# Batch 0 of a fused attention and softplus MLP: plain products, w_in stored once in fp32, fewer loads, and a new order of steps

## The chip, the cores and the metric

One core of one Trainium2 chip runs the whole program. The metric is device time in microseconds for one execution, the median of several runs. The core has five engines with a queue of instructions each: PE (TensorE, matrix products), DVE (VectorE) and ACT (ScalarE) for work on elements, POOL, and SP, which here issues nearly all DMA transfers. Each engine takes its instructions strictly in order and waits at an instruction until what it needs is there, so the order in which the program was written decides who waits for whom.

## What is computed

```python
# x (8,8,512,64), state (8,8,32,64); per batch and head
scores = scale * x @ state.T;   a  = softmax(scores);   xread = a @ state     # (512, 64)
scores2 = scale * state @ x.T;  a2 = softmax(scores2);  sread = a2 @ x        # (32, 64)
rows = concat([xread, sread])          # heads side by side: (8 * 544, 512)
h = rows @ w_in                        # (4352, 2048), w_in 512 x 2048
g = softplus(h)
out = g @ w_out                        # w_out 2048 x 512
```

The weights arrive as 64-bit floats and are turned into fp32 on the chip. An fp32 product is made from rounded parts (fp32r): each operand is split into a high part and a remainder, and three products high*high, high*low, low*high are summed.

## The kernel before

The first 512 rows of a batch (`xread`) go through the MLP batch by batch; the 32 `sread` rows of all eight batches form a ninth batch, number 8. `xread` itself is not built: `h = a @ (state @ w_in)`, so each batch has state products `V.b.c` (c is one of four column chunks of w_in, made by `B.V...`) and hidden tiles `h.b.f` (f = 0 to 15, 128 rows of hidden units by 512 tokens, six matmuls each: two groups of heads by three part products). For batches 4 to 7 the state products are made stacked (`B.K...`), written to DRAM (`vd`) and read back rearranged (`Lv`).

The second product runs as sweeps: batch b, half s of 256 tokens. A sweep has eight units u (two hidden tiles each), and a unit is a 2x2 block product with seven products in place of eight: `sfa`, `sfb`, `sfc` on DVE build sums of softplus blocks, `gh` (ACT) and `gl` (DVE) split seven blocks of 128 columns (896 wide) into parts, and `p.b.s.u.0` to `.3` are the PE steps (three of six 128x256 matmuls into the PSUM tiles `pk_X`, `pk_Y`, `pk_Z`, one of a 512- and a 256-wide matmul into `pk_Q`). `e1` to `e6` combine the banks and `So` stores the rows. W_out must be put in its own seven forms first (`cfa` to `cfd`, `wh`/`wl`, `Th`/`Tl`, `Eh`/`El`).

The softplus values of batches 0 to 7 are written to DRAM in whole tiles (`Td`, buffer `td`) and read back per sweep (`Tr`). For `sread`, each group of heads g of a batch has row maxima (`E`), exponentials (`e`), a transpose on DVE (`H`), a store (`Se`, buffer `te`), four rearranging loads per group (`Le.b.g.j`), two loads of x (`Lx`, from `in_xn`), and then the reads `B.Rb` on PE (tile `rp`). Batch 8 needs w_in itself in parts: `uh`/`ul` split it, `Su` stores the two parts (buffer `ud`), `Lu` loads them again before `h.8`.

The order of everything is the table `PLAN`: one entry `name:engine:place` per step, emitted one by one, so each engine's queue is this order with the other engines left out. `place` numbers PSUM banks or slots of SBUF. `w.i` are warm-up transposes of no use to the result. The helper lines are L323 (ACT copies and casts of `split` and `copy`), L339 (DVE subtractions of `split`), L330 and L333 (loads, stores), L342 (matmuls of `mm`), L736, L737, L740 (products of a sweep).

Of the kernel before, what the change touches and what calls it, by code (L numbers as in the profile page):

```python
# [42 lines left out]
PLAN = """
Lt.0.1:S:16 Lt.0.0:S:18 Lz.0:S:20 Li.0.0:S:22 Li.0.1:S:24 Lt.1.1:S:26 Lz.1:S:21 Lt.1.0:S:28 Li.0.3:S:30 Li.0.2:S:32 Li.1.3:S:34 Li.1.0:S:36 B.Q0:T:0,1
qk.0.0.0:A:38 qk.0.0.1:V: qk.0.1:A:39 w.0:T:3 A2.0.0:T:2 Sq.0.0:S: ch.0.0:A:40 Sq.0.1:S: ch.0.1:A:41 cu.0.0:V:42 Li.1.1:S:44 A.0.1:T:3 cr.0.0:V: A2.0.1:T:4
M.0.1:V: A.0.0:T:5 cu.0.1:V:46 Li.1.2:S:48 Ms.0.1:T: M.0.0:V: cr.0.1:V: Ms.0.0:T: m.0.1:A:50 N.0.1:V: V.0.0.0.0:T:6,7 m.0.0:A:51 V.0.0.0.1:T: ch.0.3:A:52
N.0.0:V: B.Q1:T:0,1 vf.0.0:A:53 vf.1.0:A:54 ch.0.2:A:55 Nm.0.1:V: qk.1.1:A:56 Nm.0.0:V: w.1:T:2 w.2:T:2 D.0.1:T:3 qk.1.0:A:57 Sq.1.1:S: cu.0.3:V: D.0.0:T:5
ch.1.3:A:58 Li.2.0:S:60 cu.0.2:V: A.1.1:T:4 ac.0.1:V:59 Li.2.1:S:62 ac.0.0:A:64 A.1.0:T:2 Sq.1.0:S: M.1.1:V: ch.1.0:A:65 h.0.1.0:T:1 cr.0.2:V: ah.0.0:A:66
Lq.0.1:S:68 h.0.1.1:T: ah.0.1:A:70 Ms.1.1:V:69 uh.0.0:A:72 cr.0.3:V: h.0.0.0:T:0 m.1.1:A: M.1.0:V: ch.1.1:A:55 h.0.0.1:T: N.1.1:V: s.0.0.1:A:74 V.0.0.1.0:T:
Ms.1.0:V:52 V.0.0.1.1:T: Nm.1.1:V: B.V1.0:T:3,5 vf.0.1:A: vf.1.1:V: m.1.0:A: cu.1.0:V:76 Li.2.2:S:78 h.0.2.0:T:4 cu.1.1:V: Li.2.3:S:80 cr.1.0:V: h.0.2.1:T:  # L50
cr.1.1:V: vh.1.0.0:A:82 N.1.0:V: h.0.3.0:T:2 vh.1.0.1:A:84 ch.1.2:A:65 h.0.3.1:T: E.0.1:V: s.0.0.0:A: D.1.1:T:1 Nm.1.0:V: vl.1.0.0:V: D.1.0:T:6 vl.1.0.1:V:
ah.1.1:A:86 Td.0.0:S: cu.1.2:V:88 ah.1.0:A:90 Li.3.0:S:92 al.1.1:V: s.0.1.0:A:94 al.1.0:V: s.0.1.1:A: cu.1.3:V: Li.3.1:S:96 ch.2.0:C:69 h.1.2:T:7 cr.1.2:V:
Td.0.1:S: ch.2.1:C:16 cr.1.3:V: ch.2.2:C:17 h.1.3:T:3 Lo.0:S:18 al.0.0:V: s.1.1.0:A:22 Lo.1:S:24 al.0.1:V: ch.2.3:C:40 cu.2.0:W:26 Li.3.2:S:28
B.V0.1+V1.1:T:0,5,1,4 ch.3.0:C:41 cu.2.1:W: Li.3.3:S:30 s.1.1.1:A: uh.0.1:A:32 Td.1.1:S: cr.2.0:V: ch.3.1:C:50 h.1.1:T:6 Lt.2.0:S:38 cr.2.1:V: vh.1.1.0:A:36
Lt.2.1:S:44 cu.2.2:W:56 Lt.3.0:S:54 vh.1.1.1:A:52 Lt.3.1:S:48 vh.0.1.0:A:34 vl.1.1.0:V: h.1.0:T:2 Lz.2:S:51 vh.0.1.1:A:64 vl.1.1.1:V: Lk.0:S:69 s.1.0.1:A:74
# [879 lines left out]
```

## Time and profile before

| what | us |
|---|---|
| median of 3 runs (lowest, highest) | 662.86 (662.17, 666.21) |
| the profiled execution, its own time | 663.22 |
| its span, from the first to the last instruction | 661.4 |
| PE busy in it, matmuls | 622.9 (94%) |
| DVE busy | 515.6 (78%) |
| ACT busy | 389.2 (59%) |
| moved by DMA | 157.88 MB, 239 GB/s on average |

PEld in the rows below is PE's loading of weights. Busy time of PE counts matmuls from their start to a modelled end, and neighbours overlap; the cost of one matmul in a stream is the distance between two starts. Idle time of an engine counts only where the work that ends last waits for it.

### The profile page before, as it was taken

Reading aid. Unit: us, or ns where it says so; the run is one execution under the profiler, and the core shown is the slowest. Engines: PE = TensorE matmul, PEld = TensorE weight load, DVE = VectorE, ACT = ScalarE, POOL = GpSimd, SP = SyncE. Lnnn points to the kernel's source line nnn. Section 1 sums busy time; section 2 is a strip of 40 time slices with the busy share of each in tenths; the row PEclk is TensorE's granted clock in tenths of the full one; section 3 lists DMA queues with packets and bytes.
Section 4 is the critical chain, followed back from the end, with each engine's and each line's share of the span. In section 5 each row is a group of like instructions: output and inputs, shape, how many; then the busy total and the mean of one; then the engine's idle time right before and its main releaser. Section 6 shows DMA issues by size and latency. Waiting matters only on the chain.

```text
span 661.4 us, 12889 instructions
## 1 busy us (share of the span) xinstructions
PE 622.9 (94%) x4710; PEld 540.1 (82%) x4710; DVE 515.6 (78%) x1126; ACT 389.2 (59%) x622; POOL 1.0 (0%) x7
## 2 busy tenths in 40 slices
...
PEclk9999999998999998999897999999999999999999
...
GB/s 332 334 383 412 358 300 367 374 348 368 343 310 145 203 223 228 271 189 255 229 208 218 170 230 218 197 224 169 182 218 231 251 211 159 224 203 35 145 48 33
DMA packets 73599, 157.88 MB, mean 239 GB/s; under 512 B 9536, under 2 KB 19776, under 8 KB 73536
## 3 DMA queue, kind: packets, MB, share of 16 engines
...
q10 hardware_dynamic: 288, 0.66, 0.3%
...
## 4 chain that ended last, share of the span: by engine, by line
PE 51%; DMA 21%; DVE 16%; ACT 5%; issue 3%; SPq 3%; DVEq 0%; ACTq 0%
PE pk_X L740 11%; PE h L342 10%; PE pk_Y L740 10%; PE pk_Z L740 10%; DVE arena L339 7%; DMA arena<-in_w_in_dram 4%; DMA arena<-in_xn_dram 4%; PE pk_Q L736 3%; ACT arena L323 3%; DMA arena<-td 2%; SPq L330 2%; PE h L794 2%; DMA vd<-arena 2%; DMA arena<-vd 2%; DMA td<-arena 2%
## 5 line engine op out<-in xcount | busy, mean ns | idle before, releaser
L323 ACT CAST arena<-arena 128x896 fp32r<-128x896 f32 (+2 forms) x231 | 180.4, 805 | 188.9 <-DVE arena L721 99.4
L339 DVE TENSOR_TENSOR arena<-arena,arena 128x896 fp32r<-128x896 f32 (+2 forms) x231 | 206.3, 912 | 56.5 <-ACT arena L323 53.7
L342 PE MATMUL h<-arena,arena 128*128 128x512 f32 x760 | 194.1, 404 | 10.4 <-ACT arena L693 4.0
L342 PEld LDWEIGHTS h<-arena,arena 128*128 128x128 f32 x760 | 140.3, 191 | 54.7 <-ACT arena L323 7.1
L740 PE MATMUL pk_Y<-arena,arena 128*128 128x256 f32 x816 | 122.0, 285 | 4.3 <-ACT arena L323 3.8
L740 PE MATMUL pk_X<-arena,arena 128*128 128x256 f32 x816 | 121.5, 285 | 0.2 <-DVE arena L339 0.2
L740 PE MATMUL pk_Z<-arena,arena 128*128 128x256 f32 x792 | 119.7, 287 | 0.4 <-DVE arena L747 0.4
L740 PEld LDWEIGHTS pk_X<-arena,arena 128*128 128x128 f32 x816 | 110.3, 191 | 9.6 <-ACT arena L323 0.8
L740 PEld LDWEIGHTS pk_Y<-arena,arena 128*128 128x128 f32 x816 | 108.6, 192 | 5.3 <-ACT arena L323 4.2
L740 PEld LDWEIGHTS pk_Z<-arena,arena 128*128 128x128 f32 x792 | 106.3, 194 | 2.0 <-issue 1.2
L718 DVE TENSOR_TENSOR arena<-arena 128x256 f32<-128x256 f32 x136 | 56.6, 420 | 48.0 <-DMA arena<-td 45.3
L693 ACT ACTIVATE arena<-h 128x512 f32<-128x512 f32 x128 | 74.5, 609 | 21.1 <-PE h L342 16.1
L736 PE MATMUL pk_Q<-arena,arena 128*128 128x512 f32 x128 | 51.5, 403 | 0.2 <-DVE arena L339 0.2
L721 DVE TENSOR_TENSOR arena<-arena 128x128 f32<-128x128 f32 x136 | 38.3, 287 | 1.6
L720 DVE TENSOR_TENSOR arena<-arena 128x128 f32<-128x128 f32 x136 | 37.9, 285 | 1.2
L737 PE MATMUL pk_Q<-arena,arena 128*128 128x256 f32 x128 | 36.0, 281 | 0.0
L342 PE MATMUL rp<-arena,arena 128*32 128x64 f32 x512 | 13.2, 266 | 15.4 <-DMA arena<-te 10.2
L342 PEld LDWEIGHTS rp<-arena,arena 128*32 128x32 f32 x512 | 10.9, 139 | 17.9 <-DMA arena<-te 10.3
L736 PEld LDWEIGHTS pk_Q<-arena,arena 128*128 128x128 f32 x128 | 24.6, 192 | 0.6 <-DVE arena L339 0.4
L737 PEld LDWEIGHTS pk_Q<-arena,arena 128*128 128x128 f32 x128 | 24.6, 192 | 0.0
L693 ACT ACT_TABLE_LOAD x18 | 23.1, 1283 | 1.5 <-PE h L342 1.2
L794 PE MATMUL h<-sreadT,arena 128*128 128x512 f32 x64 | 23.0, 393 | 0.0
...
## 6 DMA issues: line engine op xcount, KB each, us to landing
td<-arena SPq DMA_DIRECT2D x64, 512.0 KB, 4.4
arena<-td SPq DMA_DIRECT2D x128, 256.0 KB, 3.7
arena<-in_w_in_dram SPq DMA_DIRECT2D x16, 512.0 KB, 8.1
arena<-in_w_out_dram SPq DMA_DIRECT2D x16, 512.0 KB, 7.6
ud<-arena SPq DMA_DIRECT2D x16, 512.0 KB, 5.2
...
arena<-vd SPq DMA_DIRECT2D x128, 64.0 KB, 3.4
arena<-in_xn_dram SPq DMA_DIRECT2D x16, 512.0 KB, 6.8
```

The source lines that it names most:

```text
L323: nc.scalar.copy(dst, src)
L330: op(name, "S", list(ins), outs, lambda e: (nc.scalar if name in BYACT else nc.sync).dma_start(dst(), src()))
L339: lambda e: eng(e).tensor_tensor(r(dlo()), src(), dhi(), ALU.subtract))
L342: nc.tensor.matmul(dst, lhs, rhs, start=start, stop=stop)
L693: nc.scalar.activation(t[:, :, 0::3] if i == 0 else t[:, :, 1:3], src.rearrange("p (s c t) -> p s c t", s=2, t=P), AF.Softplus)
L718: op(f"sfa.{k}", "V", t, [f"t.{k}:a"], lambda e, g=blocks: nc.vector.tensor_tensor(g()[:, 0:2], g()[:, 4:7:2], g()[:, 7:8].broadcast_to([P ...
L720: op(f"sfb.{k}", "V", [t[0], f"t.{k}:a"], [f"t.{k}:b"], lambda e, g=blocks: nc.vector.tensor_tensor(g()[:, 2], g()[:, 1], g()[:, 4], ALU.add))
L721: op(f"sfc.{k}", "V", [t[1], f"t.{k}:b"], [f"t.{k}:c"], lambda e, g=blocks: nc.vector.tensor_tensor(g()[:, 3], g()[:, 5], g()[:, 2], ALU.s ...
L736: nc.tensor.matmul(at(bank), g(0), r(wform(u, m)(slice(0, 2))), start=first, stop=False, skip_group_check=True)
L737: nc.tensor.matmul(at(bank)[:, 0:256], g(1), r(wform(u, m)(0)), start=False, stop=True, skip_group_check=True)
L740: nc.tensor.matmul(at(bank)[:, 256 * half:256 * half + 256], g(gi), r(wform(u, m)(wi)), start=first and pi == ps[0] and i == 0, stop=i == ...
L794: nc.tensor.matmul(hb, r(w[:, 0, cs]), r(at("sreadT")[:, :, kt, :]), start=kt == 0, stop=False, skip_group_check=True)
```

## The change

Batch 0 no longer uses sweeps. Its hidden tiles are softened in one ACT instruction each (`s.0.f`), split (`gh.0.f`, `gl.0.f`, 512 wide, buffer `g`), kept in SBUF, and multiplied plainly: `m.0.f.c` adds three 128x512 matmuls to the accumulator of 128 rows c, in two turns (f 0 to 3, f 4 to 15); after the first the four accumulators are copied out (`o.0.0.c`), after the second added (`o.0.1.c`) and stored. Batch 0's `Td` and `Tr` are gone. Since the plain product needs W_out unchanged, `T1` is now split into W_out's slot after its last plain use (`Wh`, `Wl`), eight halves more.

w_in goes to DRAM as fp32 (`Sf`, buffer `fd`, eight stores of 512 KB) instead of as two parts (`Su`), is loaded in eight loads (`Lf`) and split again (`xh`, `xl`) for batch 8. `Le` loads both groups of a batch at once (32 issues where there were 64), `Lv` both halves of a chunk (64 where there were 128). `B.R0+R1` and `B.R2+R3` are taken apart. All steps are in a new order.

```diff
-SPILLED = (0, 1, 2, 3, 4, 5, 6, 7)
+SPILLED = (1, 2, 3, 4, 5, 6, 7)
+PLAIN = (0,)
+TURNS = ((0, 0, 4), (0, 4, 16))
-SWEEPS = tuple((b, s) for b in range(B) for s in range(2)) + ((8, 0),)
+SWEEPS = tuple((b, s) for b in range(B) if b not in PLAIN for s in range(2)) + ((8, 0),)
...
-                for j in range(4):
-                    load(f"Le.{k}.{j}", [f"aT.{k}:{j}"], lambda k=k, j=j: page(f"aT.{k}", 4, P)[NS * j:NS * j + NS],
-                         lambda k=k, j=j: io.te[k].rearrange("(q t) (j e) -> j t q e", t=NS, j=4)[j], [f"D:te.{k}"])
+                if g:
+                    for j in range(4):
+                        load(f"Le.{b}.{j}", [f"aT.{b}:{j}"], lambda b=b, j=j: page(f"aT.{b}", 8, P)[NS * j:NS * j + NS],
+                             lambda b=b, j=j: io.te[b].rearrange("g (q t) (j e) -> j t (g q) e", t=NS, j=4)[j], [f"D:te.{b}.{h}" for h in range(2)])
...
+        if PLAIN:
+            used = [f"acc.{b}.{x}.{c}:{f1}" for b, x, f0, fe in RUNS if f0 <= f1 < fe for c in range(4)]
+            split(f"Wh.{u}", f"Wl.{u}", lambda c1=c1: part(c1, 1), lambda f1=f1: page(f"W.{f1}", 2, DM)[:, 0, 256:512],
+                  lambda f1=f1: page(f"W.{f1}", 2, DM)[:, 1, 256:512], [f"{c1}:T"] + used, f"W.{f1}:Th", f"W.{f1}:Tl", "A")
...
+            def gemm2(e, acc=acc, c=c):
+                for i, (gi, wi) in enumerate(PASSES):
+                    mm(at(acc), r(page(f"g.{k}", 2, S)[:, gi, P * c:P * c + P]), r(page(f"W.{f}", 2, DM)[:, wi]), f == f0 and i == 0, f == f1 - 1 and i == 2)
...
+            store(f"Sf.{c}.{i}", whole, lambda c=c, i=i: io.fd[c, i], lambda c=c, i=i: at(f"wf.{c}.{i}"), [f"D:fd.{c}.{i}"])
+            load(f"Lf.{c}.{i}", [f"wg.{c}.{i}:"], lambda c=c, i=i: at(f"wg.{c}.{i}"), lambda c=c, i=i: io.fd[c, i], [f"D:fd.{c}.{i}"])
...
-            store(f"Su.{k}", [f"u.{k}:h", f"u.{k}:l"], lambda c=c, q=q: io.ud[c][q], lambda k=k: at(f"u.{k}"), [f"D:ud.{k}"])
-            load(f"Lu.{k}", [f"uu.{k}:h", f"uu.{k}:l"], lambda k=k: at(f"uu.{k}"), lambda c=c, q=q: io.ud[c][q], [f"D:ud.{k}"])
+            split(f"xh.{k}", f"xl.{k}", lambda c=c, q=q: page(f"wg.{c}.{q // 2}", 2, 512)[:, q % 2],
+                  lambda k=k: page(f"uu.{k}", 2, 512)[:, 0], lambda k=k: page(f"uu.{k}", 2, 512)[:, 1], [f"wg.{c}.{q // 2}:"], f"uu.{k}:h", f"uu.{k}:l", "A")
```

Where the order moves work, three places. The first is PE's queue early in the program, behind the hidden tiles 0 and 1 of batch 0 (`h_2`, `h_3` are tiles 2 and 3; `vp` are state products, `ab` are transposes of the softmax, `acc_0_c` the accumulators of the first turn). Before:

```order
L342 MATMUL h_2_418<-arena_356,arena_301 128x512
L342 MATMUL h_2_418<-arena_343,arena_317 128x512
L342 MATMUL h_3_431<-arena_356,arena_301 128x512
L342 MATMUL h_3_431<-arena_343,arena_317 128x512
L436 MATMUL ab_1_440<-ident,arena_371 128x128 x4
L436 MATMUL ab_0_447<-ident,arena_301 128x128 x4
L342 MATMUL h_2_471<-arena_458,arena_426 128x512 x3
```

Now:

```order
L331 MATMUL h_3_398<-arena_298,arena_288 128x512
L331 MATMUL acc_0_3_407<-arena_384,arena_389 128x512 x3
L331 MATMUL h_3_398<-arena_317,arena_288 128x512
L331 MATMUL acc_0_3_407<-arena_334,arena_402 128x512 x3
L331 MATMUL acc_0_1_428<-arena_384,arena_389 128x512 x3
L331 MATMUL acc_0_1_428<-arena_334,arena_402 128x512 x3
L331 MATMUL acc_0_0_440<-arena_384,arena_389 128x512 x3
L331 MATMUL acc_0_3_407<-arena_425,arena_419 128x512 x3
```

The sixteen plain products of the first turn have moved in between, and the hidden tiles of batch 1 (the last row of before) come behind them. The second place is where the last hidden tiles of batch 3 end on PE. Before, tiles of batch 4 and then batch 0's first unit follow:

```order
L342 MATMUL h_7_1904<-arena_1423,arena_573 128x512 x3
L342 MATMUL h_7_1904<-arena_1233,arena_1519 128x512 x3
L740 MATMUL pk_0_X<-arena_773,arena_1698 128x256 x3
L740 MATMUL pk_0_X<-arena_841,arena_1698 128x256 x3
L740 MATMUL pk_0_Y<-arena_773,arena_1698 128x256 x3
L740 MATMUL pk_0_Y<-arena_841,arena_1698 128x256 x3
```

Now the second turn, 48 rows of accumulators `acc_1_c` of which the first two and the last stand here, and then batch 1's first unit:

```order
L331 MATMUL h_15_1793<-arena_1170,arena_1223 128x512 x3
L331 MATMUL h_15_1793<-arena_594,arena_1223 128x512 x3
L331 MATMUL acc_1_0_1805<-arena_1619,arena_870 128x512 x3
L331 MATMUL acc_1_1_1815<-arena_1619,arena_870 128x512 x3
...
L331 MATMUL acc_1_3_1827<-arena_1978,arena_1967 128x512 x3
L766 MATMUL pk_0_X<-arena_384,arena_2025 128x256 x3
```

All hidden tiles of batch 4 have moved behind this point. The third place is SP's queue ahead of the reads of batches 0 and 1 (`te` numbers are per batch and group before, per batch now). Before, from the store of batch 1's second group to the last load of the pair of reads:

```order
L333 DMA te_69<-arena_2766 128x512
L330 DMA arena_1856<-te_67 32x4x128 x2
L330 DMA arena_285<-td_114 128x512
L330 DMA arena_1856<-te_67 32x4x128 x2
L330 DMA arena_1112<-in_xn_dram 128x1024
L330 DMA arena_2766<-in_xn_dram 128x1024
L330 DMA arena_2534<-in_xn_dram 128x1024
L330 DMA arena_1856<-te_66 32x4x128 x2
L330 DMA arena_1950<-in_xn_dram 128x1024
L330 DMA arena_1856<-te_66 32x4x128 x2
L330 DMA arena_414<-te_68 32x4x128 x4
L330 DMA arena_414<-te_69 32x4x128 x4
```

Now, the same from batch 1's second store to the loads of its own read:

```order
L322 DMA te_67<-arena_2338 128x512
L319 DMA arena_2347<-td_101 128x512
L319 DMA arena_767<-in_xn_dram 128x1024
L319 DMA arena_330<-in_xn_dram 128x1024
L319 DMA arena_2338<-te_67 32x8x128 x4
```

Batch 0's loads now stand earlier, before batch 1's stores, with a read of their own.

## Rows read from the trace of the kernel before

**Rows 1.** Page, span in 40 slices: granted PE clock in tenths.
```profile
PEclk9999999998999998999897999999999999999999
```
**Rows 2.** By stage: busy (x) of PE, PEld, DVE, ACT, POOL; PEclk, DMA, GB/s.
```profile
0.00:33.50 33.50, 28.10 (x186) 16.85 (x186) 23.72 (x51) 24.00 (x40) 1.01 (x7) 1.00 0.90 331
33.50:157.70 124.20, 116.64 (x718) 79.14 (x718) 100.77 (x204) 106.66 (x197) 0.00 (x0) 0.98 0.97 364
157.70:427.40 269.70, 248.43 (x2060) 225.46 (x2059) 219.79 (x505) 164.11 (x246) 0.00 (x0) 0.95 0.70 233
427.40:661.40 234.00, 229.68 (x1751) 218.66 (x1749) 171.32 (x370) 94.42 (x142) 0.00 (x0) 1.00 0.50 166
```
**Rows 3.** PE timeline at 442 us: start, us, line, operation, count [idle before <-releaser].
```profile
442.70 0.89 PE L740 MATMUL pk_X<-arena,arena 128*128 128x256 f32 x6
443.42 0.88 PE L740 MATMUL pk_Y<-arena,arena 128*128 128x256 f32 x6
...
444.86 0.40 PE L736 MATMUL pk_Q<-arena,arena 128*128 128x512 f32 x1
445.10 0.28 PE L737 MATMUL pk_Q<-arena,arena 128*128 128x256 f32 x1
445.21 1.56 PE L342 MATMUL h<-arena,arena 128*128 128x512 f32 x6
446.61 0.86 PE L740 MATMUL pk_X<-arena,arena 128*128 128x256 f32 x6
```
**Rows 4.** PE timeline at 33 us: the pair B.V0.1+V1.1 and what follows.
```profile
33.54 1.95 PE L342 MATMUL vp<-arena,arena 64*32 64x512 f32 x32
35.42 2.79 PE L342 MATMUL h<-arena,arena 128*128 128x512 f32 x11
```
**Rows 5.** Chain that ended last, pieces in order of time: start, us, what.
```profile
122.95 1.59 PE vq L342 x12
...
398.12 1.02 PE sc L342 x16
...
418.18 1.03 PE rp L342 x64
```
**Rows 6.** PE timeline: first product of batch 4, and the last products of all.
```profile
427.39 0.88 PE L740 MATMUL pk_X<-arena,arena 128*128 128x256 f32 x6
...
656.57 0.52 PE L740 MATMUL pk_Q<-arena,arena 128*128 128x256 f32 x3
```
**Rows 7.** PE timeline at batch 0's first product and around PE's waits.
```profile
168.94 0.88 PE L740 MATMUL pk_X<-arena,arena 128*128 128x256 f32 x6
...
195.68 0.38 PE L740 MATMUL pk_Y<-arena,arena 128*128 128x256 f32 x1 [3.79 <-ACT arena L323]
...
258.02 0.28 PE L737 MATMUL pk_Q<-arena,arena 128*128 128x256 f32 x1
...
265.72 1.66 PE L342 MATMUL h<-arena,arena 128*128 128x512 f32 x6
...
308.79 0.88 PE L740 MATMUL pk_Y<-arena,arena 128*128 128x256 f32 x6
...
316.93 1.44 PE L740 MATMUL pk_Z<-arena,arena 128*128 128x256 f32 x5
...
340.37 0.88 PE L740 MATMUL pk_Y<-arena,arena 128*128 128x256 f32 x6
...
351.52 1.65 PE L740 MATMUL pk_Z<-arena,arena 128*128 128x256 f32 x6
```
**Rows 8.** Tile rp (reads): what its engine waited for, us in total, times.
```profile
  DMA arena<-te: 20.5, 9
```
**Rows 9.** Page, DMA issues: count, KB each, us from issue to landing.
```profile
td<-arena SPq DMA_DIRECT2D x64, 512.0 KB, 4.4
...
ud<-arena SPq DMA_DIRECT2D x16, 512.0 KB, 5.2
```
**Rows 10.** SP's queue ahead of the reads R0+R1: start, us, issues merged.
```profile
254.03 8.06 SPq L330 DMA_DIRECT2D arena<-te  x10
```

More of the change, by code (lines that the diff above doesn't have):

```diff
@@ L48 @@
[L48 to L55, printed above, removed]
@@ L276 @@
+p.7.1.7.4:T: e4.7.1:V: e5.7.1:V: So.7.1.0:S: e7.7.1:V: So.7.1.1:S: e6.7.1:V: So.7.1.2:S: So.7.1.3:S:
 """
@@ L296, in width @@
     kind = buf.split(".")[0]
-    if kind in ("vp", "sc", "st", "ab", "ss", "rp", "tp", "h", "wp", "vq", "pk"):
+    if kind in ("vp", "sc", "st", "ab", "ss", "rp", "tp", "h", "wp", "vq", "pk", "acc"):
         return 0
@@ L302, in rounded @@
 def rounded(buf):
-    return buf.split(".")[0] in ("V", "a", "W", "u", "K", "G", "F", "uu", "E")
+    return buf.split(".")[0] in ("V", "a", "W", "u", "K", "G", "F", "uu", "E", "g")
 def graph(io, at, nc):
@@ L573, in f @@
                     for q in range(4):
-                        mm(at(f"rp.{b}")[NS * q:NS * q + NS, D * g:D * g + D], page(f"aT.{b}.{g}", 4, 4, NS)[:, q, c],
+                        mm(at(f"rp.{b}")[NS * q:NS * q + NS, D * g:D * g + D], page(f"aT.{b}", 8, 4, NS)[:, 4 * g + q, c],
                            page(f"x.{b}.{q // 2}", 4, 4, D)[:, c, 2 * (q % 2) + g], c == 0, c == 3)
-        return [f"aT.{b}.{g}:{j}" for g in range(2) for j in range(4)] + [f"x.{b}.{i}" for i in range(2)], [f"rp.{b}"], f
+        return [f"aT.{b}:{j}" for j in range(4)] + [f"x.{b}.{i}" for i in range(2)], [f"rp.{b}"], f
     def stacked(c, q):
@@ L648, in graph, with plain @@
             hidden(b, f)
+    def plain(b, f, x, f0, f1):
+        k = f"{b}.{f}"
+        op(f"s.{k}", "A", [f"h.{k}:0"], [f"tq.{k}"], lambda e: nc.scalar.activation(at(f"tq.{k}"), at(f"h.{k}"), AF.Softplus))
+        split(f"gh.{k}", f"gl.{k}", lambda: at(f"tq.{k}"), lambda: page(f"g.{k}", 2, S)[:, 0], lambda: page(f"g.{k}", 2, S)[:, 1],
+              [f"tq.{k}"], f"g.{k}:h", f"g.{k}:l", "A")
+        for c in range(4):
+            acc = f"acc.{b}.{x}.{c}"
+            def gemm2(e, acc=acc, c=c):
+                for i, (gi, wi) in enumerate(PASSES):
+                    mm(at(acc), r(page(f"g.{k}", 2, S)[:, gi, P * c:P * c + P]), r(page(f"W.{f}", 2, DM)[:, wi]), f == f0 and i == 0, f == f1 - 1 and i == 2)
+            op(f"m.{k}.{c}", "T", [f"g.{k}:h", f"g.{k}:l", f"W.{f}:h", f"W.{f}:l"] + ([f"{acc}:{f - 1}"] if f > f0 else []), [f"{acc}:{f}"], gemm2)
+    for b, x, f0, f1 in RUNS:
+        for f in range(f0, f1):
+            plain(b, f, x, f0, f1)
+        for c in range(4):
+            acc, o = f"acc.{b}.{x}.{c}", f"o.{b}.{c}"
+            if x == 0:
+                op(f"o.{b}.{x}.{c}", "AV", [f"{acc}:{f1 - 1}"], [f"{o}:{x}"], lambda e, o=o, acc=acc: copy(e, at(o), at(acc)))
+            else:
+                op(f"o.{b}.{x}.{c}", "V", [f"{acc}:{f1 - 1}", f"{o}:{x - 1}"], [f"{o}:{x}"],
+                   lambda e, o=o, acc=acc: nc.vector.tensor_tensor(at(o), at(acc), at(o), ALU.add))
+            if f1 == NFT:
+                store(f"So.{b}.{c}", [f"{o}:{x}"], lambda b=b, c=c: io.out[b * ROWS + P * c:b * ROWS + P * c + P], lambda o=o: at(o))
     for i in range(2):
```

477 lines of the change are left out of this document (237 added, 240 removed).

## Prediction

> **What bounds the kernel now.** I read the busy shares by stage first, then the PE (TensorE) rows for the time that each kind of work takes when nothing is waited for, then the gaps that the PE rows leave.
>
> By stage the kernel has three parts [rows 2]. Up to about 158 us the DMA engines are full (share 0.90, then 0.97 at 364 GB/s; the clock's digits are in [rows 1]), PE is busy 116.6 of 124.2 us, ACT 106.7, DVE 100.8: four things close to full. From 158 to 427 us DMA falls to 0.70 and nothing is full, yet PE is idle 21 us and its clock averages 0.95. From 427 us on PE is busy without a gap at full clock. So the end is set by PE: the time at which PE's work begins to flow, what is left then, and what it waits for on the way.
>
> The price of PE work is read where PE never waits, from one start to the next [rows 3]: six 128x256 products 0.72 us (442.70 to 443.42), the pair that makes the seventh product 0.24 + 0.11 us, one hidden tile `h` of six 128x512 products 1.40 us (445.21 to 446.61). A unit `p.b.s.u` of a seven-product sweep is 442.70 to 445.21, 2.51 us. A pair of state products `B.V` is 1.88 us [rows 4], a pair of `B.K` 1.59, a `B.Q` 1.02, a read `B.R` 1.03 [rows 5].
>
> These prices hold: from p.4.0.0.0, at 427.39 us, 72 units (180.7), 34 `h` (47.6) and one read are left, 229.4 us, which ends at 656.8. The profile's last product starts at 656.57 and two more of 0.12 follow it [rows 6]. Behind it the program needs 4.5 us to its end at 661.4.
>
> The same count from h.4.0 (eight `h`, 11.2 us, ahead of the first product of batch 0 at 168.94 [rows 7]: 157.7 us) gives 17 sweeps 341.5, 80 `h` 112.0, eight reads 8.2, three `B.Q` 3.1, in all 464.8 us, where 499.2 pass. **34.4 us are lost** between 157.7 and 427, and the rows say where. Three groups of reads hold PE [rows 7]: R0+R1 from 258.14 to 265.72, R5 from 309.51 to 316.93, R2+R3 from 341.09 to 351.52; less their own work (2.06, 1.03, 2.06) that is 5.5 + 6.4 + 8.4 = 20.3 us. The waits of reads are mostly for loads from `te` [rows 8]. A wait for a W_out split ahead of 195.68 costs 3.8 [rows 7]. The clock's digits below 9, each a stretch at half clock (1.2 of 2.4 GHz), stand in the slices of these waits [rows 1], and what follows a wait runs slowly for a while. That and pieces below 1 us are the other 10.3.
>
> **The change, part by part.** *PE work.* Batch 0 was 16 units of 2.51 us, 40.2 us. Plain it is 64 products `m`, each three 128x512 matmuls at 0.233 (half of an `h`, 0.70 us): 44.8 us, so +4.6. Eleven more warm-up pairs of 128x128 transposes are put in, eight of them between two `m` that depend on late W_out parts; in a wait they cost nothing, without one at most two 128x256 products each, 0.24 us, 2.6 in all. I charge nothing, and the upper bound below takes them in.
>
> *PE's place of the work.* Sixteen `m` (f 0 to 3) now stand ahead of B.V0.1+V1.1, the other 48 behind the last `h` of batch 3, ahead of everything of batch 4. Before h.4.0 nothing else of batch 0 is on PE.
>
> *DMA.* Batch 0's 8 stores and 16 loads of `td` go (8.4 MB at 512 KB and 256 KB each); w_in is kept once in fp32 instead of as two parts, so 16 stores and 16 loads of 512 KB become 8 and 8 (8.4 MB less) [rows 9]. `Lv` goes from 128 issues to 64 and `Le` from 64 to 32, with the same bytes. Issues fall from 596 to 460.
>
> *Stage one, to the pair B.V0.1+V1.1, at 33.5 us now.* It gains 16 `m` and one `h`: 11.2 + 1.4 = 12.6 us of PE, and 37 issues of DMA stand ahead of it where 30 stood. W_out tiles 0 to 3 must be loaded, converted and split ahead of the `m`s. Below: 33.5 + 12.6 = 46, with the idle of the stage unchanged; above 50, if each of the four f waits another 1 us or the warm-up pairs are paid. I take 48, since the order gives the first `m` only 1 to 3 us behind their splits.
>
> *Stage two, from there to the last `h` of batch 3, 33.5 to 157.7 us now.* PE has 58 `h` (81.2), seven `B.V` pairs (13.2), eight `B.K` pairs (12.7) and three `B.Q` (3.1): 110.2 of 124.2 us, 14 lost at a DMA share of 0.97. After, one `h` less and two warm-ups, 109.5. The issues in it are now 32 `vd` stores, 29 `td` stores, 16 `ud` stores, 24 `Lv`, 10 tiles of W_out and 24 others; after, the same `vd` stores, 21 `td`, 4 `fd`, 2 `Lv`, 8 W_out tiles and 16 others. By sizes as in [rows 9] that is 46.6 MB, 128 us at the stage's 364 GB/s, so DMA lasts as long as the stage, and then 31.8 MB, 87 us. DMA is no longer the longest. What takes over is PE, 109.5, with ACT behind it: the casts of batch 0's `g` come into this stage, those of the seven-product form and of the second parts leave it. Below: 111 us, PE with hardly a wait; above 123.5, the 14 us of idle unchanged. I take 116, nearer to the lower end, since the row that filled the stage is relieved by 30%, but three other engines stay near full. So m.0.4.0 starts at 48 + 116 = **164 us** (157 to 173.5).
>
> *From there on PE has* 48 `m` 33.6, 15 sweeps 301.3, 80 `h` 112.0, reads 8.2, `B.Q` 3.1: **458.2 us** against 464.8 before.
>
> *What is lost on the way.* The 48 `m` need `g` and W_out parts that stand 5 to 20 us of PE work ahead of them in the order, so the wait ahead of 195.68 has no successor; DVE prepares W_out's forms, batch 1's first units and batch 0's last adds in the same stretch, the tightest place of the new order: 0 to 4 us. Reads: before, R0+R1 had behind the last of their stores four `xn` loads and 16 `Le`; SP issues them in order, ten of them taking 8.06 us [rows 10], and the last landed at about 265. After, R1 has two `xn` loads and four `Le`, under a third as many issues, with 11 us of PE work between its store and itself; the other reads have 11 to 17 us and six transfers each. At half a us an issue and the 3 to 8 us that a landing takes that fits, so I keep 4 us of the 20.3. Of the 10.3 us of slow clock and pieces, 7 stay. With 2 for DVE: **13 us** (5, if only half of the pieces stay, to 34.4, if nothing is gained).
>
> *Splits that are added.* 16 casts on ACT and 16 subtractions on DVE for the reloaded w_in, and eight halves of W_out. They lie beside PE in the last part, where ACT is busy 94.4 us with 142 instructions (0.66 each) and DVE 171.3 of 234 [rows 2]; DVE also loses batch 0's combining and wide splits. Charged at nothing; without that cover 16 x 0.66 = 10.6 us.
>
> **A rule against the rows.** One product of 512 columns takes 0.233 us from start to start behind another [rows 3]. The Trainium skill, "TensorE: Matmul & The Clock Gate", section "Back-to-back issue gap", says that a stream of weight loads and matmuls sustains about 131 ns for N=512. By that batch 0's plain products would be an estimated 192 x 0.131 = 25.2 us instead of 44.8 and the sum 19.6 us lower. The rows do not bear it out, and the sum goes by them.
>
> **The sum.** 164 + 458.2 + 13 + 4.5 = 639.7 us of span. The profiled execution spans 661.4 and the median of the runs is 662.86, 1.5 above it: 641.2; I round to **641 us**.
>
> **Rivals.**
> - *Only the reads gain* (stage two keeps its 14 us of idle because ACT, DVE and PE hand work to each other, whatever DMA does): m.0.4.0 at 173.5, 649.2 span, 651 us. For it: ACT is busy 86% of the stage [rows 2].
> - *Only the start gains* (SP still issues in order, and a read still waits for its `te` loads): 34.4 in place of 13, 661.1 span, 662.6 us, no change. Against it: two thirds of the issues between store and read are gone.
> - *The stalls move and none goes* (slower). PE's idle is a property of the hand-offs; both stages keep it and the 4.6 us of plain work and the waits for W_out tiles come on top: 173.5 + 458.2 + 34.4 + 4.5 = 670.6, 672 us, 1.4% slower. It decides from a start of m.0.4.0 behind 171 us with the reads waiting as before.
> - *Everything flows*: 157 + 458.2 + 5 + 4.5 = 624.7, 626 us.
> - *Matmuls of 512 columns are cheap in a long run*: one of 512 costs no more than one of 256, 0.12 us, once a long run has no other work in it: 192 x 0.12 = 23.0 in place of 44.8, 619 us. Against it stand the six products of an `h`, back to back at 0.233 [rows 3]. The Trainium skill's page above is what speaks for it.
>
> **How the numbers follow.** Forecast 0.50, only reads 0.16, only start 0.14, stalls move 0.10, everything flows 0.08, cheap products 0.02. The range leaves out the two ends: 626 to 663. A change under 1% (6.6 us) can hardly be told from none here. Faster by over 1% (below 656.2) are the forecast, the reads alone, everything flows and cheap products, 0.76; same 0.14; slower 0.10.
>
> **What the profile after would show.** Right: the DMA share of 50 to 150 us well below 0.97; the long run of `acc` matmuls starting at 157 to 170 us without a gap; reads that hold PE for about their own 1.03 us; PE flowing from there with clock 1.00. Wrong: `acc` rows waiting for DVE or ACT in the first 50 us, `acc` starting behind 171 us, gaps of 3 us or more at `rp` released by `te` loads, or a new place between 160 and 350 us where PE waits for DVE.

## The result, and the profile after

| | us |
|---|---|
| kernel before, median of 4 runs (lowest, highest) | 664.54 (662.17, 666.52) |
| changed kernel, median of 4 runs (lowest, highest) | 632.69 (628.89, 636.10) |
| ratio, 95% interval | 0.9521 (0.9453, 0.9588) |
| the forecast, its range | 641 (626 to 663) |
| profiled execution of the changed kernel, its span | 633.1, 631.3 |

The page of the changed kernel, the span in 40 slices: the granted clock of PE and the busy share of DMA, in tenths.
```profile
PEclk9999999999999999999999999999999999999999
DMA  9969766669906669968799857863848574431411
DMA packets 64253, 141.07 MB, mean 223 GB/s; under 512 B 7360, under 2 KB 17600, under 8 KB 64192
```
No slice's clock is below nine tenths, where [rows 1] has four such slices, and of DMA's seven digits from 47 to 158 us only the first and the last are still 9. The bytes fell from 157.88 to 141.07 MB.

By stage, columns as in [rows 2]. The stages end at the same work as there: the pair B.V0.1+V1.1, the first product behind batch 3's last `h` (now m.0.4.0), the first product of batch 4.
```profile
0.00:48.30 48.30, 45.20 (x258) 29.77 (x259) 35.31 (x75) 34.55 (x61) 1.00 (x7) 1.00 0.85 327
48.30:159.70 111.40, 110.78 (x716) 76.35 (x716) 88.65 (x173) 102.23 (x187) 0.00 (x0) 1.00 0.77 284
159.70:381.60 221.90, 216.06 (x1750) 193.73 (x1749) 187.69 (x423) 138.43 (x224) 0.00 (x0) 1.00 0.74 234
381.60:631.30 249.70, 244.92 (x1885) 230.34 (x1883) 192.39 (x412) 122.02 (x189) 0.00 (x0) 1.00 0.52 167
```
Stage two has 0.6 us of idle PE, where it had 7.6 by the same columns, and its DMA share is 0.77 instead of 0.97. At the prediction's prices, which are those of full clock, 1.9 us are lost there now (111.4 less 109.5) and 14.0 were lost before. Batch 4 starts 45.8 us earlier (381.6 against 427.4), and has more work behind it than before only because sweeps and `h` stand in another order.

What PE waited for: us in total, times, longest. First the reads alone in the kernel before, 157 to 430 us, then all of the changed kernel, 160 to 430 us.
```profile
PE rp L342 <- DMA arena<-te: 10.2, 5, 4.7
PE rp L342 <- DMA arena<-in_xn_dram: 2.9, 1, 2.9
PE rp L342 <- issue: 2.3, 2, 1.2
```
```profile
PE sc L331 <- DMA arena<-in_zp_dram: 2.1, 1, 2.1
PE rp L331 <- DMA td<-arena: 1.5, 1, 1.5
PE rp L331 <- DMA out_dram<-arena: 1.0, 1, 1.0
PE tp L539 <- ACT arena L536: 0.5, 1, 0.5
...
PE rp L331 <- issue: 0.2, 1, 0.2
```
Of the reads' 15.4 us of idle PE (the 20.3 of the prediction hold slow stretches and pieces too) 2.7 us are left, at R4, R1 and R0. The names td and out_dram are those of transfers that landed at the same moment; R4's last load from `te` landed at 253.17, R4 starts at 253.41. What is new is the first row: B.Q6 waits for the small load of batch 6's `zp`.

PE around R4 and R0, as in [rows 3].
```profile
250.99 0.88 PE L766 MATMUL pk_Y<-arena,arena 128*128 128x256 f32 x6
253.41 1.10 PE L331 MATMUL rp<-arena,arena 128*32 128x64 f32 x64 [1.54 <-DMA td<-arena]
254.44 1.66 PE L331 MATMUL h<-arena,arena 128*128 128x512 f32 x6
...
264.87 0.88 PE L766 MATMUL pk_Z<-arena,arena 128*128 128x256 f32 x6
265.97 1.10 PE L331 MATMUL rp<-arena,arena 128*32 128x64 f32 x64 [0.21 <-issue]
```
A read now takes its own 1.03 us from start to start, and what follows it runs at once at full speed.

**Where the 30.1 us of span went.** Both profiles have one point from which only PE's work and its waits are left: h.4.0 at 157.7 before, m.0.4.0 at 159.7 after. It comes 2.0 us later; behind it stand 457.2 us of work instead of 464.8 (the 48 `m` took 32.6), 9.9 us lost instead of 34.4, and the same tail of 4.5 (the last three products start at 626.45, in [rows 6] at 656.57): 2.0 - 7.6 - 24.5 = -30.1. The 12.6 us that sixteen `m` and one `h` add to stage one are paid by stage two, which is 12.8 shorter (111.4 against 124.2): 12.1 us less are lost and 0.7 us of work have left it.

### The profile page after: what moved, and what is told of

Same layout as the page of the kernel before. It is cut to its first block, busy times and chain, and to the rows that moved or that the text cites. A ratio compares the mean times of both kernels' runs of the same rounds, so it can differ in the third digit from the quotient of the medians.

```text
span 631.3 us, 12414 instructions
## 1 busy us (share of the span) xinstructions
PE 617.0 (98%) x4604; PEld 530.2 (84%) x4604; DVE 504.0 (80%) x1081; ACT 397.2 (63%) x659; POOL 1.0 (0%) x7
## 2 busy tenths in 40 slices
DMA packets 64253, 141.07 MB, mean 223 GB/s; under 512 B 7360, under 2 KB 17600, under 8 KB 64192
## 4 chain that ended last, share of the span: by engine, by line
PE 70%; DVE 14%; DMA 10%; issue 2%; ACT 2%; SPq 2%; DVEq 0%; ACTq 0%
PE h L331 21%; PE pk_X L766 9%; PE pk_Y L766 9%; PE pk_Z L766 9%; PE acc L331 7%; DVE arena L328 4%; DMA arena<-td 3%; PE pk_Q L762 3%; PE h L820 2%; PE vp L331 2%; DMA arena<-vd 2%; PE vq L331 2%; SPq L319 1%; DVE arena L744 1%; PE pk_Q L763 1%
## 5 line engine op out<-in xcount | busy, mean ns | idle before, releaser
L312 ACT CAST arena<-arena 128x512 fp32r<-128x512 f32 (+2 forms) x255 | 185.8, 763 | 140.2 <-DVE arena L747 46.5
L328 DVE TENSOR_TENSOR arena<-arena,arena 128x512 fp32r<-128x512 f32 (+2 forms) x255 | 213.5, 858 | 58.3 <-ACT arena L312 56.1
L766 PE MATMUL pk_Y<-arena,arena 128*128 128x256 f32 x720 | 106.2, 284 | 0.4 <-DVE arena L328 0.4
L766 PE MATMUL pk_X<-arena,arena 128*128 128x256 f32 x720 | 105.5, 283 | 0.0
L766 PE MATMUL pk_Z<-arena,arena 128*128 128x256 f32 x696 | 103.8, 284 | 0.4 <-DVE arena L328 0.4
L766 PEld LDWEIGHTS pk_X<-arena,arena 128*128 128x128 f32 x720 | 96.6, 189 | 5.9
L766 PEld LDWEIGHTS pk_Z<-arena,arena 128*128 128x128 f32 x696 | 92.2, 191 | 1.8 <-issue 0.8
L331 PE MATMUL acc<-arena,arena 128*128 128x512 f32 x192 | 45.7, 396 | 0.0
L331 PEld LDWEIGHTS acc<-arena,arena 128*128 128x128 f32 x192 | 35.8, 188 | 8.1 <-issue 1.0
L378 DVE SCALAR_TENSOR_TENSOR arena<-arena,arena 128x512 int32<-128x512 int32 x31 | 21.0, 688 | 0.5
```

The lines of the kernel that those rows point to most:

```text
L312: nc.scalar.copy(dst, src)
L328: lambda e: eng(e).tensor_tensor(r(dlo()), src(), dhi(), ALU.subtract))
L378: nc.vector.scalar_tensor_tensor(u, h2().bitcast(I32), 3, u, ALU.logical_shift_left, ALU.bitwise_or)
L766: nc.tensor.matmul(at(bank)[:, 256 * half:256 * half + 256], g(gi), r(wform(u, m)(wi)), start=first and pi == ps[0] and i == 0, stop=i == ...
```

## Experiments

Each kernel is the one before or the changed one with one edit. Times are medians, and the ratio is to the kernel before on the same chip.

### Was DMA's volume what held PE in stage two?

Before, with half of each early `td` store:
```diff
-  store(Td.b.u: io.td[b, u] <- tt.b.u)
+  n = 512 if b < 4 else 1024
+  store(Td.b.u: io.td[b, u][:, 0:n] <- tt.b.u[:, 0:n])
```


> The kernel before, with the td stores of batches 0 to 3 cut to their first half (256 KB instead of 512) and the second sweep of these batches reading the first half again: the second half of their tokens is computed from the first half's hidden tiles, all instructions of PE, ACT and DVE and all issues stay. About 7.6 MB less in stage two (46.6 to 39.0 MB, 107 us at 364 GB/s, below the 110.2 us of PE work). Theory volume: h.4.0 starts at 148 to 152 instead of 157.7, and since the reads keep their waits, the time falls by 5 to 10 us (about 653 to 658). Rival hand-offs: h.4.0 at 156 to 159 and the time within 3 us of the kernel before.

651.43 us, ratio 0.9841 (0.9800 to 0.9881). Its stage two, to the time at which h.4.0 starts now (147.82):
```profile
33.50:147.80 114.30, 113.39 (x725) 77.87 (x724) 100.69 (x204) 106.76 (x197) 0.00 (x0) 1.00 0.90 331
```
PE is idle 0.9 us of 114.3, and h.4.0 comes 9.8 us earlier with all the work of ACT, DVE and PE unchanged. In this execution the stage begins at 35.27, 1.7 us later, so by itself it lasts 112.6 us instead of 124.1. SP issues 594 transfers in both kernels, so only the bytes differ. The reads keep their waits, and the end comes 11 us earlier, a little more than expected. So with all issues kept, fewer bytes are enough to end the idle time: it was volume. Part of its effect is that a shorter store frees its place in SP's queue sooner (the next question): SP waits 12.4 us for places in this stage instead of 19.9.

The other way round, the changed kernel with `td` stores issued twice, and then with the `vd` stores twice as well:
```diff
   dma(io.td[b, u] <- tt.b.u)
+  if b < 4: dma(io.tx[b, u] <- tt.b.u)
```


> The changed kernel, with each of the 24 td stores of batches 1 to 3 (512 KB) issued a second time into a spare DRAM tile: 12.6 MB and 24 issues more, nearly all of it between 48 and 160 us; the output is unchanged. Theory volume (the 14 us of PE's idle in stage two were there because DMA was full): 31.6 MB + 11 to 12.6 MB at the 364 GB/s of the kernel before are 117 to 121 us, longer than the 111.4 us that the stage lasts, so PE gets its idle back: m.0.4.0 starts at 167 to 172 instead of 159.7, the DMA share of the stage is above 0.93, and the time is 8 to 13 us over the changed kernel's, about 641 to 646. Rival hand-offs (ACT, DVE and PE set the idle, whatever DMA does): m.0.4.0 at 158 to 162, the time within 3 us of the changed kernel's 632.7.

> The changed kernel with the td stores of batches 1 to 3 and all 32 vd stores issued twice, the second time into spare DRAM tiles: 21 MB and 56 issues more; the output is unchanged. With the td stores alone doubled, 7 MB more moved between 48 and 160 us (share 0.90, 346 GB/s) and PE did not feel it; the vd stores bring the stage to about 46.6 MB, what the kernel before had there. Theory volume: 46.6 MB at 364 GB/s are 128 us, so m.0.4.0 starts at 168 to 178 instead of 159.7, the DMA share of 50 to 155 us is 0.95 or more, and the time is 644 to 654. Rival hand-offs: m.0.4.0 at 158 to 163 although the share is near full, and the time 636 to 640, as with the td stores alone.

With `td` twice: 636.45 us (0.9608), m.0.4.0 at 159.40. With both: 656.89 us (0.9928, 0.9899 to 0.9957), m.0.4.0 at 170.96. Stage two of the first and of the second, cut at 48.3 as above:
```profile
48.30:159.70 111.40, 110.02 (x692) 76.19 (x685) 84.40 (x162) 97.90 (x180) 0.00 (x0) 1.00 0.90 346
```
```profile
48.30:170.90 122.60, 113.68 (x694) 76.69 (x683) 81.52 (x156) 94.81 (x172) 0.00 (x0) 0.99 0.93 356
```
Both are best read against the unchanged kernel's second profile (the 632.00 us below), since in all three the stage begins at 46.8. At a share of 0.90 PE loses 1.2 us in the stage (m.0.4.0 at 159.40 against 158.16): the first expectation missed because only 7 of the 12.6 MB fell into it (346 against 284 GB/s for 111.4 us). More comes behind: p.1.1.0.0 starts 7.2 us later (227.76 against 220.57), of which 4.4 are left at the end. At 0.93 PE loses 12.8 us in the stage, and by p.1.1.0.0 25 us (245.88). The stores that did not fit run on into the plain sweep: its DMA share is 0.90 (171.0 to 210.7 us), where the unchanged kernel has 0.46. The time is above the 644 to 654 that "volume" expected. These two kernels have 24 and 56 issues more as well as the bytes, so only the half stores show the bytes by themselves. The relief is real, and the changed kernel stands not far from the edge.

### What held the reads, and what released them?

The changed kernel with its `Le` and `Lv` loads cut into two issues each again, and with the `Le` alone:
```diff
-  load(Le.b.j: aT.b[rows j] <- io.te[b], both halves g)
+  for h in range(2): dma(aT.b[rows j, half h] <- io.te[b], half h)
```


> The changed kernel, with each Le load issued as two (one for each te half, 32 issues to 64) and each Lv load as two (64 to 128), as the kernel before had them; the place of the reads in PE's order is that of the changed kernel. Theory issues: the last Le of each read lands 2 to 4 us later, the six reads before 420 us then wait 1 to 3 us each, 6 to 15 us in all, with some half clock behind it: 640 to 650. Theory place (the new order gives the reads 11 to 17 us of PE work behind their stores): 0 to 4 us, 633 to 637.

> The changed kernel with only the 32 Le loads issued as two each (64 issues; Lv stays at 64). With Le and Lv both split the time was 649.1 and at most eight transfers of SP's queue were under way at any time, so that an issue waits until the eighth before it has landed. Theory own loads (a read waits for its own Le, and eight of them instead of four stand right ahead of it): most of the 16 us, 641 to 647. Theory all slots (every issue takes one of the eight places for the 3 to 6 us until it lands, whoever waits for it): about a third, as 32 of the 96 issues, 636 to 640.

Both split: 649.14 us (0.9794, 0.9762 to 0.9826). `Le` alone: 639.04 us (0.9627, 0.9592 to 0.9663), beside 632.00 for the unchanged kernel on the same chip. So 96 issues more, with the same bytes and PE's order untouched, give back about 17 of the 32 us, and 32 of them 7. (The bytes also go in smaller pieces: 67839 DMA packets with both split, 64253 unchanged.) Both split, what PE waited for from 160 to 430 us:
```profile
PE rp L331 <- DMA arena<-te: 5.2, 4, 1.9
PE sc L331 <- DMA arena<-in_zp_dram: 3.7, 1, 3.7
PE pk_X L773 <- DVE arena L328: 2.7, 3, 1.7
PE tp L543 <- ACT arena L540: 1.9, 1, 1.9
PE pk_Y L773 <- DVE arena L328: 1.3, 1, 1.3
PE pk_Q L769 <- DVE arena L780: 1.1, 1, 1.1
...
```
Only 5.2 us of it are reads, against 2.7 unchanged and 15.4 in the kernel before; with `Le` alone split it is 2.3. So most of what the reads gained does not come from fewer issues. What else the new order changed for them is their place on PE, which the next question takes up, and that R0+R1 and R2+R3 are apart, with two `x` loads ahead of a read instead of four; what that is worth by itself was not run. The rest of the loss is what SP issues behind the `Le` and `Lv`: batch 6's `zp`, and the `td` loads, for which DVE waits 25.4 us instead of 15.7. The time is in the range of "issues", but not by the waits of reads that it counted on.

Why an issue costs so much is in SP's rows. One price is handing it over, 0.41 to 0.42 us at the median in all these kernels: from 160 to 430 us 108.9 us for 230 issues unchanged, 130.7 for 285 with both split. The other is a place. In the kernel before and in the changed one no issue of SP starts with more than seven of its transfers under way; 130 of the 594 start with exactly seven before, 82 of 458 after. Ahead of R0+R1, inside [rows 10], `Le` issues start at 255.27, 256.94 and 259.13, and the `x` loads issued eight issues earlier land at 255.21, 256.92 and 259.11. Of the 8.06 us of [rows 10], 4.0 are four waits like these and 4.1 the ten issues themselves. One row of what SP waited for in the kernel before, 157 to 430 us (the largest row, 25.2 us, is a wait for DVE and not for a place):
```profile
SPq L330 <- DMA arena<-in_xn_dram: 16.7, 13, 2.1
```
The issue that waits has nothing to do with that `x` load. The trace names the place: SP's transfers use eight semaphores in turn, and the wait is for the one that the issue itself will use. So an issue takes one of eight places until it has landed. The same row from 160 to 430 us in the changed kernel, with `Le` split, and with both split:
```profile
SPq L319 <- DMA arena<-in_xn_dram: 2.6, 2, 1.9
```
```profile
SPq L529 <- DMA arena<-in_xn_dram: 13.3, 8, 2.5
```
```profile
SPq L529 <- DMA arena<-in_xn_dram: 13.5, 11, 2.0
```
All waits of SP for the semaphore of its own next issue, counted in the trace over the same stretch, are 33.5 us in the kernel before, 7.0 in the changed one, 17.2 with `Le` split and 20.6 with both. For half the bytes a place is held 0.8 (`te`) and 0.6 (`vd`) of the time. The loads of 160 to 430 us, both split and unchanged: KB each, median us to landing.
```profile
arena<-vd SPq DMA_DIRECT2D x82, 64.0 KB, 2.5
...
arena<-te SPq DMA_DIRECT2D x56, 64.0 KB, 4.7
```
```profile
arena<-vd SPq DMA_DIRECT2D x49, 128.0 KB, 4.2
...
arena<-te SPq DMA_DIRECT2D x28, 128.0 KB, 5.6
```
With `Le` alone the 7.0 us lie within the 636 to 640 of "all slots", and as the 64 issues of `Lv` cost about 10 us more, a read's own loads are not all that counts. That the places are all of it isn't shown: with `Le` split the waits for them grow by 10 us and the handing over by 8, with `Lv` split as well by 3 and by 14 more. No run parts the two prices.

Then fewer issues should help the kernel before. Its four `Lv` loads of a part as one:
```diff
-  for q in range(4): load(vr.b.c.o[rows q] <- io.vd[c, o][q, own])
+  load(vr.b.c.o <- io.vd[c, o][:, own])
```


> The kernel before with the four Lv loads of each vd part made one (128 issues to 32, the same bytes and rows, issued where the last of the four stood); PE's order and the Le loads untouched. In the changed kernel 96 issues more (64 Lv and 32 Le) cost 16 us. Theory issues (SP's in-order queue sets when loads land between 200 and 430 us): 96 fewer take 6 to 14 us off: 649 to 657, most of it between 240 and 360 us, R2+R3 waiting 3 us or more less, because eight Lv issues stand between its own loads. Rival own loads (only the Le and x loads right ahead of a read count): 0 to 4 us, 659 to 663.

689.42 us, 1.0413 (1.0375 to 1.0452): 27 us slower, a miss of both expectations. The load of 256 KB is the slow part: it lands 5.2 us behind its issue at the quickest, where a 64 KB load has 1.8, and ACT waits 39.9 us in 17 places for loads from `vd` instead of 18.3 in 11. Stretches of 1 us in which the second load of a pair is about all that is under way (issued at 221.52, its cast at 231.09), columns as in [rows 2]:
```profile
229.00:230.00 1.00, 1.00 (x9) 0.94 (x8) 0.93 (x4) 0.34 (x1) 0.00 (x0) 1.00 0.26 100
230.00:231.00 1.00, 1.00 (x6) 0.80 (x5) 0.37 (x1) 0.00 (x0) 0.00 (x0) 1.00 0.26 98
```
The DMA share is 0.26, about 4 of the 16 engines, at 98 to 100 GB/s. The Trainium skill, "DMA: Bandwidth & Descriptors", section "Why a DMA increments its semaphore by 16 and not by 1", says that a DMA runs on the largest number of engines up to 16 that divides the slowest dimension on both sides. The merged load's slowest dimension in DRAM is the four q, so by that rule it runs on four engines, and the trace agrees with 0.26; the loads that it replaces have 32 rows. The edit thus changed two things, the count and the width, and also the place (it is issued where the last of the four stood). It says nothing about the count alone, and what fewer issues, of `Lv` or of `Le`, would give the kernel before stays open.

The last run on this question takes `Lv` off SP, in the changed kernel:
```diff
-  nc.sync.dma_start(Lv...)
+  nc.gpsimd.dma_start(Lv...)
```


> The changed kernel with its 64 Lv loads issued by GpSimd instead of SP; the same transfers, everything else in its order. Theory issues: SP's other loads go out earlier, the waits that are left (R4 1.7 us, R1 1.2, Q6 2.2, T.3 0.7, Z 0.6) shrink by 3 to 5 us in all: 627 to 631. Rival latency (what is left is the time of a store and a load): 632 to 634. If GpSimd's issues come late or slowly, vh and the hidden tiles h.5 to h.7 behind them are late: above 636.

638.55 us (0.9630, 0.9587 to 0.9674). SP starts 45 issues instead of 82 with seven under way and waits 1.1 us for places from 160 to 430 us instead of 7.0, so the places are freed, and it does not help. One part is seen: the four loads for vh.5.1 are issued about half a us earlier (the last at 293.36 instead of 293.83), but the last lands at 299.53 instead of 296.78. vh.5.1.0 starts at 299.62 instead of 296.87, and h.5.4 behind it waits.
```profile
PE h L331 <- ACT arena L312: 2.0, 1, 2.0
```
The expectation "late or slow" fits, as a slow landing; the other 4 us come in steps of at most 2.1 us, whose cause was not followed. The profile lists these loads under another kind of queue (`software_dynamic`), so the run changes more than the places, and it doesn't show what freed places alone would give.

### What does a waiting read cost?

R0, R2 and R5 moved on PE to right behind their last `Le`:
```diff
-  Le.0.3 gl.2.0.3 p.2.0.2.0 ... p.2.0.3.2 B.R0
+  Le.0.3 B.R0 gl.2.0.3 p.2.0.2.0 ... p.2.0.3.2
```


> The changed kernel with the reads R0, R2 and R5 put on PE right behind the issue of their last te load: 5.0, 6.5 and 6.5 us of PE work earlier, everything else in its order. In the changed kernel their last loads land at 265.9, 322.4 and 345.5 us, so they wait about 5, 5 and 5.5 us more than now. Theory waits (a wait of a read is paid at the end, one for one, and the clock falls behind it): 632.7 + 15 us, with half-clock stretches behind the waits another 2 to 5 us: 646 to 653. Rival slack (what stands behind gets ahead meanwhile, so that the waits at Q6, R5 and T.3 go): 636 to 641.

650.51 us (0.9827, 0.9793 to 0.9861), within "waits". PE waits 5.0, 5.3 and 5.8 us at the three, close to the 5.0, 6.5 and 6.5 us that they were moved by: it is their place on PE that keeps the reads from waiting. The first:
```profile
257.37 1.56 PE L331 MATMUL h<-arena,arena 128*128 128x512 f32 x6
263.75 1.93 PE L331 MATMUL rp<-arena,arena 128*32 128x64 f32 x64 [4.82 <-DMA arena<-td]
265.61 1.65 PE L766 MATMUL pk_X<-arena,arena 128*128 128x256 f32 x6
267.06 1.48 PE L766 MATMUL pk_Y<-arena,arena 128*128 128x256 f32 x6
268.34 1.48 PE L766 MATMUL pk_Z<-arena,arena 128*128 128x256 f32 x6
```
From 263.7 to 269 the granted clock is 0.50, that is 1.2 GHz. The read takes 1.86 us instead of 1.03 and the next three steps 1.45, 1.28 and 1.28 instead of 0.72: 2.7 us on top of the wait. At p.4.0.0.0 the kernel is 17.0 us behind the unchanged one (397.01 against 380.05 in the second profile) and stays there. The three waits are 16.1; 5.1 of waits that the unchanged kernel has (R0 1.5, R1 0.6, Q6 2.1, T.3 0.9) are in that or go; the remaining 6 us are three times the slow clock. A wait of a read is paid at the end, and the clock adds to it.

### What was charged at nothing: the warm-up pairs

```diff
-  w.3 ... w.13 (eleven pairs of transposes)
```


> The changed kernel without its eleven new warm-up pairs (w.3 to w.13); all other work in its order. Theory cover (eight of them stand in a wait, the other three cost at most 0.7 us, and the clock does not hang on them): 631 to 634, clock 1.00 from 10 us on. Rival clock (the 3.5 us of waiting ahead of m.0.3.3 then bring half clock, as such waits did in the kernel before): a stretch at half clock of some 3 us from about 41 us on, and 1 to 3 us more: 634 to 636.

> The changed kernel once more, unchanged, so that the kernels of this call have it beside them on the same chip: 630 to 635, ratio to the kernel before 0.950 to 0.956.

630.86 us (0.9521) beside 632.00 (0.9519) for the unchanged kernel: the same. Without the pairs h.1.0 starts at 40.13 instead of 42.61, so they do cost 2.5 us where they stand. Eight of them run in one row, in the changed kernel's first profile:
```profile
37.21 3.85 PE L615 MATMUL wp<-ident 128*128 128x128 f32 x16
40.82 0.94 PE L331 MATMUL acc<-arena,arena 128*128 128x512 f32 x3
```
That is 0.45 us a pair from start to start. Without them PE is idle 1.0 us there, and full clock does not hang on them:
```profile
30.00:40.00 10.00, 8.88 (x41) 6.63 (x40) 9.83 (x25) 9.97 (x20) 0.00 (x0) 1.00 1.01 367
```
The 2.5 us are still there at m.0.4.0 (155.66 against 158.16) and p.4.0.0.0 (377.12 against 380.05), and all but 0.8 gone at p.5.0.0.0 (439.04 against 439.80). They go here:
```profile
421.97 0.74 PE L765 MATMUL pk_Z<-arena,arena 128*128 128x256 f32 x4 [1.91 <-DVE arena L327]
...
423.15 2.77 PE L765 MATMUL pk_Y<-arena,arena 128*128 128x256 f32 x12
```
p.4.1.4 waits for its `gl`, which stands on DVE behind a sum that waits for its `td` load (landed at 419.81); the granted clock of 419.6 to 427 is 0.77.

### Can the order be bettered?

First nearly every place at which the changed kernel's PE still waits (in short):
```diff
-  gh.0.2 wh.2 ch.o3 ... ch.1.3 s.0.3 wh.3 gh.0.3      (ACT)
+  gh.0.2 wh.2 s.0.3 gh.0.3 ch.o3 ... wh.3 ch.1.0 ...
-  w.4 ... w.11 m.0.3.3      B.R4 h.4.12      B.R1 h.5.3      B.Q6 h.5.11      (PE)
+  m.0.3.3                   h.4.12 B.R4      h.5.3 B.R1      h.5.11 B.Q6
```


> The changed kernel, reordered where its trace still shows PE waiting: the casts and subtractions for m.0.3 stand earlier on ACT and DVE (s.0.3, gh.0.3, wh.3, gl.0.3, wl.3), with D.1.0 and D.1.1 behind m.0.3's first products and the adds that batch 1 waits for ahead of W_out's; ten warm-up pairs gone; R4 behind h.4.12, R1 behind h.5.3, Q6 behind h.5.11. Theory PE bound: stage one ends 3 to 4 us earlier (B.V0.1+V1.1 at about 44.5 instead of 48.3), stage two 0.6 us shorter, 1.4 + 1.2 + 1.4 us less waiting at R4, R1 and Q6: 624 to 628, ratio to the changed kernel 0.987 to 0.993. Rival give-back (what comes earlier meets loads that do not: the waits move to the next reads and units): 630 to 634.

632.97 us (0.9540, 0.9515 to 0.9565): nothing gained. The pair B.V0.1+V1.1 starts at 42.99, better than expected, and the next `h` then waits:
```profile
49.44 1.01 PE L330 MATMUL h<-arena,arena 128*128 128x512 f32 x2 [2.91 <-ACT arena L311]
```
m.0.4.0 is at 158.58, and from p.1.0.0.0 to p.4.0.0.0 it takes 189.1 us instead of 189.3: what R4, R1 and Q6 no longer wait is waited for at R0 and at p.3.0.6.0. So only the places that hold what is behind them were reordered, on top of leaving out the warm-ups (the zp load and unit 3.0.6 as told in the expectation):
```diff
-  w.3 ... w.13      B.R4 h.4.12      B.Q6 h.5.11      (PE)
+                    h.4.12 B.R4      h.5.11 B.Q6
-  gh.4.1.4 sfa.4.1.6 sfb.4.1.6 sfc.4.1.6 gl.4.1.4 gl.4.1.5      (DVE and ACT)
+  gh.4.1.4 gl.4.1.4 gl.4.1.5 sfa.4.1.6 sfb.4.1.6 sfc.4.1.6
```


> The changed kernel without the eleven new warm-up pairs, and with the three places reordered at which the trace of that version loses what it has gained: h.4.12 ahead of R4; the zp load of batch 6 three issues earlier and h.5.11 ahead of Q6, with sfc and gl of unit 3.0.6 ahead of the row maxima of other batches; and on DVE gl.4.1.4 and gl.4.1.5 ahead of sfa.4.1.6, which waits for its td load there. Without the warm-up pairs p.4.0.0.0 started 2.9 us earlier (377.1), and a wait of 2.1 us at p.4.1.4 with some 3 us of half clock behind it gave that back. Theory order (the give-back is DVE's order, not the loads): p.5.0.0.0 at 434 to 437 instead of 439.8, no half clock between 415 and 430, 626 to 629 in all. Rival loads (SP's loads set the pace up to 425 us, whatever is ahead on PE): p.5.0.0.0 at 438 to 441 and 630 to 634.

628.99 us (0.9500, 0.9469 to 0.9532; six runs from 628.50 to 630.59), 3.0 below the 632.00 of the changed kernel, which ran on another chip; by the ratios (0.9500 against 0.9519) it is 0.2%. The intervals of the two ratios overlap, so the times do not part them; the profiles differ by more. p.5.0.0.0 starts at 435.75 instead of 439.80, and from 415 to 435 us the clock is whole:
```profile
415.00:435.00 20.00, 19.07 (x131) 17.03 (x130) 14.54 (x35) 14.26 (x21) 0.00 (x0) 1.00 0.56 178
```
Between p.4.1.4 and p.5.0.0.0, then, the give-back was DVE's order, not the loads. Not all of it is mended: p.4.0.0.0 to p.5.0.0.0 takes 60.4 us, where the kernel without the pairs takes 61.9 and the unchanged one 59.8.

## Why the prediction was right, and which of its sizes were off

The span was forecast at 639.7 and is 631.3. The 8.4 us are stage two 4.6, the loss on the way 3.1 and the plain products 1.0, less 0.3 in stage one.

- *Stage one, 48.* 48.3, and 46.8 in the second profile. Right, though not in its parts: the warm-up pairs, charged at nothing, cost 2.5 us there. They were inside the upper bound, but a pair took 0.45 us and not 0.24, and the 8 that "cost nothing in a wait" stood in a wait that was shorter than they are. The sign named as wrong, `m` products that wait for ACT and DVE in the first 50 us, shows at m.0.3.3 when the pairs are out (1.0 us). Without them the stage ends at 44.3, below the lower bound of 46, so that 48 came out is in part luck.
- *Stage two, 116.* 111.4, nearly the lower bound of 111. This is the larger miss. The argument (DMA full at 0.97, relieved by 30%, PE next) held: 31.8 MB were forecast and 284 GB/s for 111.4 us are 31.6, and the half stores moved the stage with the volume alone; the doubled stores moved it back, with more issues as well. What was too cautious is the step "three other engines stay near full": ACT is busy 102 of 111 us and holds nothing. High shares of several engines did not mean that they block each other.
- *The work behind, 458.2.* 457.2. An `m` took 0.68, three products of 512 columns at 0.227 each. By the 131 ns of the Trainium skill, "TensorE: Matmul & The Clock Gate", section "Back-to-back issue gap", the 48 `m` would take an estimated 18.9 us. The 32.6 measured do not agree with it, so the rows were right to go by.
- *Lost on the way, 13.* 9.9. Reads 2.7 where 4 were kept; DVE 0.8 where 2; no half clock at all where it was part of 7. The wait ahead of 195.68 has no successor, as said. Not foreseen: 2.1 us at Q6.
- *Why the reads stop waiting.* The conclusion held, the mechanism was half right. The prediction took two reasons together, fewer issues and more PE work between a store and its read. The runs give most to the second: with the issues put back the reads wait 5.2 us, and with three of them moved forward on PE those three wait 16.1. "Half a us an issue" is the time that SP takes to hand one over; it left out the waits for one of the eight places, as long again in [rows 10]. The edit that the prediction treated as a detail of the reads (fewer, larger `Le` and `Lv`) is worth about 17 us, hardly any of it at the reads, because every other load of 160 to 430 us stands behind these issues in SP's queue. That part was priced only through the reads.
- *The clock.* The 10.3 us of slow clock and pieces were to shrink to 7; about 4 of pieces are left and none of slow clock. They were not a cost of their own, but the tail of the waits: with the waits brought back (R0, R2, R5 early), half clock came back with them, 2.7 us behind the first.
- *Added splits, at nothing.* PE waits for ACT only 0.5 us from 160 to 430 us, at T.3, and the profile has no wait of PE behind 430 us, where most of them lie.
- *Rivals.* The time lies between the forecast (641) and "everything flows" (626), which was given 0.08: m.0.4.0 at 159.7 between 164 and 157, the loss 9.9 between 13 and 5. "Only the reads gain" and "the stalls move" rested on hand-offs as the limit of stage two, which the half `td` stores showed false. "Only the start gains" was put aside because two thirds of the issues ahead of the reads are gone; with `Le` put back the time is 639, and only with `Lv` as well, for which this reason had no price, 649. So it was right in part.
